# Moving operands of both products in areas of their own, at other offsets, and three output buffers in place of four

## The chip, the cores and the metric

The kernel runs on one NeuronCore of a Trainium2 chip. The metric is the device time of one execution in microseconds (us); lower is better. A time is the median of several runs. Profiles are of one execution, taken by the hardware profiler; its span, from the first to the last instruction, is a little shorter than a timed run.

## The reference

Windowed attention with a linear bias for each head, followed by a two-layer network with a squared Relu:

```
def _attn_ref(q, k, v):                  # 8 batches, 8 heads, 576 tokens, 64 values per head
    scores = scale * np.matmul(q, k.transpose(0, 1, 3, 2))
    rel = pos[:, None] - pos[None, :]
    bias = slopes[:, None, None] * (-np.abs(rel))[None, :, :]
    mask = (rel >= 0) & (rel < 128)
    attn = softmax(np.where(mask, scores + bias[None], -1000000000.0))
    return np.matmul(attn, v)

x = attn_out.transpose(0, 2, 1, 3).reshape(4608, 512)
h = np.maximum(x @ w_in, 0.0)            # w_in: 512 x 2048
out = h * h @ w_out                      # w_out: 2048 x 512
```

## The kernel before

The 4608 tokens are cut into nine chunks of 512 (`c` from 0 to 8). A chunk's attention output is made as four tiles of 128 values by 512 tokens, one for each pair of heads (`p`). The network then runs over 16 blocks of 128 hidden values (`f`).

**The two products.** Each is done in float32r with operands split into a high and a low part, three matmuls for one product: high x high, high x low, low x high. `gemm1(c, f)` (matmul at line 194) multiplies the four input tiles of the chunk by weight block f: 4 x 3 = 12 matmuls of 128 x 128 weights by 512 moving columns, into the one PSUM bank `g`. ScalarE takes the Relu out of `g` into `r` (line 204), VectorE squares `r` (line 207), ScalarE rounds it to the high part `hh` (line 211) and VectorE writes what is left as the low part `hl` (line 213). `gemm2(c, f)` (line 223) multiplies `hh` and `hl` by the second weight block: for each of four output blocks `m`, three matmuls into the accumulator `acc[m]`, which stays open over all 16 values of f. TensorE goes through gemm1 of step n, then gemm2 of step n - 2, and so on; the attention of later chunks stands in between, at fixed steps.

**The moving operands.** In every matmul of both products the weights are the stationary operand; the moving one is a tile of 512 float32r columns, 2,048 bytes in each partition. For gemm1 these are the two halves of `xu`, a tile of `[128, 2, 512]` from a pool with eight buffers: the high part is written by a ScalarE cast (lines 301 and 477), the low part by a VectorE subtraction (lines 304 and 480). For gemm2 they are `hh` and `hl`, from a pool with three buffers of each. Pools lay their buffers one behind the other, so `xu` tiles are 4,096 bytes apart and the halves and the `hh` and `hl` tiles 2,048 bytes: all of them begin at the same place within 1,024 bytes (544 bytes past a multiple of it).

**The weights.** All 16 blocks stay in SBUF, high and low parts interleaved, so that a weight block of 128 columns is read with a step of 8 bytes from a range of 1,024. In blocks f = 0, 4, 8 and 12 the first two of the four blocks of gemm1 are stored apart, with a step of 16 bytes (`APART`).

**The output.** At f = 15, when an accumulator is complete, it is copied to an output tile `o` (line 229; VectorE for m = 0 and 2, ScalarE for m = 1 and 3), and a DMA of 256 KB writes it to HBM (line 230), on SP's queue except for the last one of the kernel, which ScalarE issues. The pool `op` of these tiles has four buffers.

**Order.** The first two chunks' worth of attention is ordered by a planner with due times (`Plan`); later steps by the tile framework's scheduler. SP's queue carries the loads of q, k and v, a round trip of the attention squares through DRAM (`way`, lines 317 and 322) and the output DMAs, in program order.

Of the kernel before, what the change touches and what calls it, by code (L numbers as in the profile page):

```python
# [9 lines left out]
F32 = mybir.dt.float32  # L10
F32R = mybir.dt.float32r
# [3 lines left out]
ALU = mybir.AluOpType  # L15
# [22 lines left out]
FIRST = 39  # L38
APART = lambda i, f, b: i == 0 and f % 4 == 0 and b < 2
CASTS = (0, 2, 15,)  # L40
COPIES = (3,)
SQUARES = (6,)
NORMS = (7,)
# [18 lines left out]
class Kern:  # L62
    def __init__(self, ctx, tc, qkd, vd, w1d, w2d, cstd, outd):
        self.tc, self.nc = tc, tc.nc
        self.qkd, self.vd = qkd, vd
        self.w1d, self.w2d, self.cstd, self.outd = w1d, w2d, cstd, outd
        ep = lambda name, bufs, **kw: ctx.enter_context(tc.tile_pool(name=name, bufs=bufs, **kw))
        self.c = ep("const", 1)
        self.ld = ep("ld", 3)
        self.tp = ep("tp", 3)  # L70
        self.pp = ep("pp", 2)
        self.sm = ep("sm", 6)
        self.xu = ep("xu", 8)
        self.hp = ep("hp", 3)
        self.op = ep("op", 4)
        self.dr = ep("dr", 4, space=bass.MemoryType.DRAM)
        self.sc = ep("sc", 1, space=PSUM)
        self.at = ep("at", 1, space=PSUM)
        self.g1 = ep("g1", 1, space=PSUM)
        self.ac = ep("ac", 4, space=PSUM)  # L80
        self.cst = self.c.tile([128, CST], F32, name="cst")
        self.ident = self.cst[:, 0:128]
        self.mask = self.cst[:, 128:192].bitcast(I32)
        self.never = self.cst[:, 192:256]
        self.raw, self.w = [None] * NF, [None] * NF
        self.nc.alloc_sbuf_tensor("arena", [128, NF * 2048], F32)
        self.arena = self.nc.sbuf_base - NF * 8192
        self.x, self.qk, self.v, self.h, self.pairs = {}, {}, {}, {}, {}
        at = lambda slot, name, shape: self.nc.alloc_sbuf_tensor_at(name, shape, F32, offset=self.arena + slot * 4096).ap()
        self.wide = [at(2 * (NF - 3), "wide", [128, H, 256])[:, 2 * p : 2 * p + 2] for p in range(NP)]  # L90
        self.room_t = [at(2 * (NF - 5) + n, f"tw{n}", [128, 4, 256]) for n in range(4)]
        self.start_banks = [self.ac.tile([128, 512], F32, name="acc") for _ in range(4)]
# [32 lines left out]
    def room(self, c, p, name, shape, offset):  # L125
        if (c, p) != (0, NP - 1):
            return self.ld.tile(shape, F32, name=name)
        at = self.arena + (NF - 1) * 8192 + offset
        return self.nc.alloc_sbuf_tensor_at(f"{name}_", shape, F32, offset=at).ap()

    def load_qk(self, c, p, sg):
        if sg == 0:
            self.qk[c, p] = self.room(c, p, "qk", [128, 1152], 0)
        to, of = self.qk[c, p], self.qkd[c, p]
        if c == 0 and sg == 0:
            to, of = (x[:, 0:768].rearrange("p (n t) -> p n t", n=2)[:, :, 0:256] for x in (to, of))
        else:
            a, e = (0, 640) if sg == 0 else (640, 1152)
            to, of = to[:, a:e], of[:, a:e]
        self.nc.sync.dma_start(to, of)  # L140
# [20 lines left out]
    def convert(self, f):  # L161
# [8 lines left out]
        yield  # L170
        (nc.gpsimd.tensor_copy if f in CASTS else nc.scalar.copy)(wh, flo)
        yield
# [13 lines left out]
    def gemm1(self, c, f):  # L186
        nc = self.nc
        xs = [self.x[c, p] for p in range(NP)]
        g = self.g1.tile([128, 512], F32, name="g")
        i = 0  # L190
        for cc in range(NCC):
            wl, wh = self.block(0, f, cc)
            for w, part in ((wh, 0), (wh, 1), (wl, 0)):
                nc.tensor.matmul(g, w, xs[cc][:, part], start=i == 0, stop=i == 11)  # L194
                i += 1
                if (c, f, i) == (0, 0, 9):
                    yield
        yield
        r = self.hp.tile([128, 512], F32, name="r", bufs=1)
        hh = self.hp.tile([128, 512], F32R, name="hh")  # L200
        hl = self.hp.tile([128, 512], F32R, name="hl")
        self.h[c, f] = hh, hl
        with self.tc.high_priority(offset=100):
            self.relu = nc.scalar.activation(r, g, AF.Relu)  # L204
        yield
        if c or f in SQUARES:
            nc.vector.tensor_tensor(r, r, r, op=ALU.mult)  # L207
        else:
            nc.scalar.activation(r, r, AF.Square)
        yield  # L210
        nc.scalar.copy(hh, r)  # L211
        yield
        nc.vector.tensor_tensor(hl, r, hh.bitcast(F32), op=ALU.subtract)  # L213
# [19 lines left out]
class Segment:  # L233
# [42 lines left out]
    def out(self):  # L276
        (self.nc.vector.tensor_copy if self.k in COPIES else self.nc.scalar.copy)(self.own, self.z)

# [17 lines left out]
    def high(self):  # L296
        K = self.K
        if self.sg == 0:
            K.x[self.c, self.p] = K.xu.tile([128, 2, 512], F32R, name="xu")
        self.u = K.x[self.c, self.p][:, :, 256 * self.sg : 256 * self.sg + 256]  # L300
        self.nc.scalar.copy(self.u[:, 0], self.X)

    def low(self):
        self.nc.vector.tensor_tensor(self.u[:, 1], self.X, self.u[:, 0].bitcast(F32), op=ALU.subtract)  # L304

# [46 lines left out]
class Couple:  # L354
# [118 lines left out]

    def high(self):
        G = self.both[0]
        self.u = self.K.x[G.c, G.p] = self.K.xu.tile([128, 2, 512], F32R, name="xu")
        self.nc.scalar.copy(self.u[:, 0], self.X)

    def low(self):
        self.nc.vector.tensor_tensor(self.u[:, 1], self.X, self.u[:, 0].bitcast(F32), op=ALU.subtract)  # L480

    def back(self):
        self.values()
# [125 lines left out]
def start(K):  # L609
# [31 lines left out]
    for k in range(8):  # L641
# [12 lines left out]
        P.add(n("z"), "PE", 0.9 * w, (n("n"),) + chain("z"), d - 3, G.turn, ("at", "zp", "pp"), "tw")  # L654
        P.add(n("o"), "DVE" if k in COPIES else "Activation", 0.6, (n("z"),), d - 2, G.out, None, "at")
        P.add(n("m"), "DVE", 0.62 if w == 1 else 0.36, (n("z"),), d + 1, G.also, None, "zp")
# [34 lines left out]
    for f in range(NF):  # L691
        d, last = CONV(f), ("w", f)
        g = K.convert(f)
        for i, (engine, us) in enumerate(CONVERT):
            if i == 3 and f in CASTS:
                engine, us = "Pool", 1.5
# [117 lines left out]
```

## Time and profile before

| | before |
|---|---|
| median of 3 runs | 955.9 us (955.64 to 956.43) |
| span of the profiled execution | 954.1 us |
| TensorE busy | 945.6 us (99%) |
| VectorE, ScalarE, GpSimd busy | 499.0, 417.5, 215.3 us |
| HBM read, written | 67.76 MB, 26.21 MB |

In the rows of the profile, PE is TensorE's matmuls, PEld its weight loads, DVE VectorE, ACT ScalarE, POOL GpSimd and SP SyncE; SPq and ACTq are the DMA issues of SyncE and ScalarE. A row of a group has its line, engine and operation, the tiles it writes and reads (out<-in), their shape and count, then busy time in us, the mean of one in ns, and the idle time of the engine ahead of it with what ended it. The duration of a matmul contains the time in which the next one is already running; what one of a stream costs is read from the distance of starts, or from the chain, where the next piece begins when the one before gives way.

### The profile page before, as it was taken

What the parts mean: (1) busy time and instruction counts of PE and PEld (TensorE: products, weight loads), DVE (VectorE), ACT (ScalarE), POOL (GpSimd) and SP (SyncE); (2) the same over time, 40 slices, a digit from 0 to 9 for tenths busy, and PEclk for the clock granted to TensorE, in tenths of its full rate; (3) what the DMA queues carried; (4) which work ended last, traced back from release to release, by engine and by line L of the source; (5) the groups of instructions that cost most, each with busy time, mean ns of one, the idle gap of its engine ahead of it and who ended that gap; (6) DMA issues with size and microseconds to landing.
All of it is one profiled execution on the core that took longest, in us unless ns stands there. A gap on an engine that the chain in (4) does not pass through costs nothing.

```text
span 954.1 us, 17229 instructions
## 1 busy us (share of the span) xinstructions
PE 945.6 (99%) x6388; PEld 795.7 (83%) x6392; DVE 499.0 (52%) x1334; ACT 417.5 (44%) x1107; POOL 215.3 (23%) x254
## 2 busy tenths in 40 slices
PE   9899999999999999999999999999999999999998
PEld 5688888888888888888888888888888888888886
DVE  6998864455545455444544454455555444433222
ACT  7898743333444444434433343344344343332222
POOL 4123331222222222222222222221212222220000
PEclk9999999999999999999999999999999999999999
DMA  9974423322433333222433232333422231111001
GB/s 348 404 274 153 146 68 119 83 66 66 124 85 83 84 88 107 73 77 73 128 83 83 74 110 72 83 83 92 119 71 72 72 96 45 45 45 45 1 1 44
DMA packets 72883, 95.10 MB, mean 100 GB/s; under 512 B 8032, under 2 KB 41952, under 8 KB 72800
## 3 DMA queue, kind: packets, MB, share of 16 engines
q1 hardware_dynamic: 72368, 93.36, 32.9%
q8 instruction: 50, 0.82, 0.4%
q10 hardware_dynamic: 432, 0.66, 0.2%
q14 instruction: 33, 0.27, 0.1%
HBM read 67.76 MB, written 26.21 MB: 98 GB/s over the span
## 4 chain that ended last, share of the span: by engine, by line
PE 95%; DMA 4%; ACT 0%; issue 0%; DVE 0%; SPq 0%; DVEq 0%
PE acc L223 42%; PE g L194 42%; PE at L338 6%; PE s L392 2%; PE g L392 2%; DMA raw<-in_dram 2%; DMA wide<-in_dram 1%; DMA qk<-in_dram 1%; PE at L392 0%; ACT raw L165 0%; ACT t L426 0%; PE acc L291 0%; ACT t L419 0%; ACT o L229 0%; DVE xu L304 0%
## 5 line engine op out<-in xcount | busy, mean ns | idle before, releaser
L194 PE MATMUL g<-xu,w 128*128 128x512 f32 x1728 | 423.2, 394 | 0.8 <-issue 0.8
L194 PEld LDWEIGHTS g<-xu,w 128*128 128x128 f32 x1728 | 344.1, 209 | 56.2 <-issue 1.7
L223 PE MATMUL acc<-hh,w 128*128 128x512 f32 x1152 | 385.9, 396 | 0.0
L223 PEld LDWEIGHTS acc<-hh,w 128*128 128x128 f32 x1152 | 223.9, 194 | 44.6 <-issue 2.4
L207 DVE TENSOR_TENSOR r<-r 128x512 f32<-128x512 f32 x129 | 104.4, 810 | 245.4 <-ACT r L204 244.2
L204 ACT ACTIVATE r<-g 128x512 f32<-128x512 f32 x144 | 85.9, 597 | 325.8 <-PE g L194 322.7
L223 PE MATMUL acc<-hl,w 128*128 128x512 f32 x576 | 226.6, 393 | 0.0
L326 POOL TENSOR_SCALAR_AFFINE_SELECT pp<-pp 128x512 f32<-128x512 f32 x128 | 107.1, 841 | 210.6 <-DMA pp<-way 171.6
L213 DVE TENSOR_TENSOR hl<-r,hh 128x512 fp32r<-128x512 f32 x144 | 109.4, 760 | 68.3 <-ACT hh L211 67.6
L262 POOL TENSOR_TENSOR t<-t,nm 128x512 f32<-128x512 f32 x64 | 82.8, 1294 | 263.5 <-DVE nm L259 155.9
L223 PEld LDWEIGHTS acc<-hl,w 128*128 128x128 f32 x576 | 112.0, 194 | 19.8
L251 ACT ACTIVATE t<-t,nm 128x128 f32<-128x128 f32 x256 | 100.0, 393 | 56.7 <-DVE nm L244 56.6
L211 ACT CAST hh<-r 128x512 fp32r<-128x512 f32 x144 | 89.0, 618 | 76.1 <-DVE r L207 74.5
L438 DVE COPY_PREDICATED t<-cst,s 64x256 f32<-64x256 int32 x100 | 44.5, 445 | 40.8 <-ACT t L426 22.4
L313 DVE STREAM_TRANSPOSE pp<-t 128x512 f32<-128x512 f32 x64 | 45.2, 707 | 38.7 <-POOL t L262 38.5
L338 PEld LDWEIGHTS at<-pp,v 128*64 128x64 f32 x1024 | 55.2, 137 | 11.2 <-issue 10.8
L338 PE MATMUL at<-pp,v 128*64 128x128 f32 x1024 | 63.0, 276 | 0.0
L244 DVE CUSTOM_DVE_ANT_0 t<-t,cst 128x128 f32<-128x128 f32 x256 | 59.0, 293 | 1.0
L251 ACT ACTIVATION_READ_ACCUMULATOR t<-t,nm 128x1 f32 x256 | 48.2, 188 | 0.0
L392 PE MATMUL s<-qk 64*64 64x64 f32 (+2 forms) x1168 | 46.3, 251 | 0.8 <-ACT raw L165 0.8
L392 PEld LDWEIGHTS s<-qk 64*64 64x64 f32 x1168 | 41.9, 133 | 1.0 <-ACT raw L165 1.0
L428 POOL MEMSET t<- 64x128 f32 (+1 forms) x44 | 9.9, 227 | 137.5 <-PE g L392 128.5
(63 smaller groups left out, 472.2 us busy)
## 6 DMA issues: line engine op xcount, KB each, us to landing
raw<-in_dram SPq DMA_DIRECT2D x32, 512.0 KB, 8.7
way<-pp SPq DMA_DIRECT2D x256, 64.0 KB, 1.8
pp<-way SPq DMA_DIRECT2D x64, 256.0 KB, 2.8
qk<-in_dram SPq DMA_DIRECT2D x32, 320.0 KB, 3.5
v<-in_dram SPq DMA_DIRECT2D x32, 320.0 KB, 2.9
qk<-in_dram SPq DMA_DIRECT2D x38, 256.0 KB, 4.1
out_dram<-o SPq DMA_DIRECT2D x35, 256.0 KB, 4.3
v<-in_dram SPq DMA_DIRECT2D x3, 256.0 KB, 4.9
```

Of the source, the lines that this page charges most:

```text
L194: nc.tensor.matmul(g, w, xs[cc][:, part], start=i == 0, stop=i == 11)
L204: self.relu = nc.scalar.activation(r, g, AF.Relu)
L207: nc.vector.tensor_tensor(r, r, r, op=ALU.mult)
L211: nc.scalar.copy(hh, r)
L213: nc.vector.tensor_tensor(hl, r, hh.bitcast(F32), op=ALU.subtract)
L223: nc.tensor.matmul(self.acc[m], w, h, start=(f == 0 and i == 0), stop=(f == NF - 1 and i == 2))
L244: self.nc.vector.tensor_tensor_reduce(self.t[:, m], self.t[:, m], self.K.nrel(2 * self.p + m // 2), -0.125, BIG, ALU.add, ALU.min, self.nm ...
L251: return self.nc.scalar.activation(self.t[:, m], self.t[:, m], AF.Exp, bias=nm[:, m : m + 1], scale=-1.0, accum_out=nm[:, 4 + m : 5 + m],)
L262: self.nc.gpsimd.tensor_tensor(self.t, self.t, self.nm[:, 8:12].unsqueeze(2).to_broadcast([128, 4, 128]), op=ALU.mult)
L326: nc.gpsimd.affine_select(to, self.own, pattern=[[-32 * sign, 4], [0, 4], [-sign, 32]], compare_op=op, fill=0.0, base=0, channel_multiplie ...
L338: self.nc.tensor.matmul(self.X[r, o : o + 128].rearrange("p (a c) -> p a c", a=4), v[:, 2 * sg + k, r], src[:, :, 2 * j + i], start=sg == ...
L392: mm = nc.tensor.matmul(to, qk[r, q0 : q0 + 64], qk[r, k0 : k0 + 64 * n], start=True, stop=True, skip_group_check=True,)
```

## The change

The `xu` pool goes. A raw area `xs` takes its place and that of `hh` and `hl`: eight slots of `XS` = 4,288 bytes for the input tiles, then six of `HS` = 2,208 bytes for the hidden ones. `new_x` puts the input tile of chunk c and pair p into slot (4c + p) % 8, and shifts it by `SHIFT[c]`; the low part begins 2,080 bytes behind the high part. `hh` and `hl` rotate over three places each, shifted by `SHIFT_H`. Since 4,288 is 4 x 1,024 + 192, 2,080 is 2 x 1,024 + 32 and 2,208 is 2 x 1,024 + 160, the tiles now begin at many different places within 1,024 bytes. Most begin at a multiple of 32 bytes; those of chunks 2 and 7 begin 16 bytes past one, those of chunk 8 begin 8 bytes past one, and `hl` in the first of its three places begins 16 past one. The number of buffers is as before, eight and three. The pool of output tiles has three buffers in place of four.

```
+SHIFT = (0, 0, 16, 32, 64, 96, 128, 48, 8)
+SHIFT_H = ((0, 16), (32, 64), (96, 128))
+XS, HS = 4160 + 128, 2080 + 128
...
-        self.xu = ep("xu", 8)
         self.hp = ep("hp", 3)
-        self.op = ep("op", 4)
+        self.op = ep("op", 3)
...
+        self.nc.alloc_sbuf_tensor("xs", [128, 2 * XS + 3 * HS // 2], F32)
+        self.xs = self.nc.sbuf_base - 8 * XS - 6 * HS
...
+    def new_x(self, c, p):
+        at = self.xs + (4 * c + p) % 8 * XS + SHIFT[c]
+        self.x[c, p] = [self.moving(f"xu{i}_{c}_{p}_", at + 2080 * i) for i in range(2)]
+
+    def moving(self, name, at):
+        t = self.nc.alloc_sbuf_tensor_at(name, [128, 520], F32R, offset=at // 32 * 32).ap()
+        return t[:, at % 32 // 4 : at % 32 // 4 + 512]
...
-                nc.tensor.matmul(g, w, xs[cc][:, part], start=i == 0, stop=i == 11)
+                nc.tensor.matmul(g, w, xs[cc][part], start=i == 0, stop=i == 11)
...
-        hh = self.hp.tile([128, 512], F32R, name="hh")
-        hl = self.hp.tile([128, 512], F32R, name="hl")
+        at, n = self.xs + 8 * XS, (16 * c + f) % 3
+        hh, hl = (self.moving(f"h{'hl'[i]}{n}_{c}_{f}_", at + (2 * n + i) * HS + SHIFT_H[n][i]) for i in range(2))
...
-        self.u = self.K.x[G.c, G.p] = self.K.xu.tile([128, 2, 512], F32R, name="xu")
-        self.nc.scalar.copy(self.u[:, 0], self.X)
+        self.K.new_x(G.c, G.p)
+        self.u = self.K.x[G.c, G.p]
+        self.nc.scalar.copy(self.u[0], self.X)
```

The order of the instructions is the same on all five engines; line numbers behind the edits grow by 12 or 13 (194 becomes 206, 223 becomes 235, 229 becomes 241, 204 becomes 216). What differs is what the output copies wait for. These rows are ScalarE's at the end of chunk 5, where the next chunk's gemm1 already runs, each with the semaphores that it waits for (DMAHW is that of a DMA queue); before:

```order
L204 ACTIVATE r<-g 128x512 [waits DVE_49,PE_49]
L229 COPY o<-acc 128x512 [waits DMAHW4_49,PE_49]
L211 CAST hh<-r 128x512 [waits DVE_49]
L229 COPY o<-acc 128x512 [waits DMAHW6_49,PE_49]
L204 ACTIVATE r<-g 128x512 [waits DVE_49,PE_49]
```

And the same rows of the changed kernel:

```order
L216 ACTIVATE r<-g 128x512 [waits DVE_49,PE_49]
L241 COPY o<-acc 128x512 [waits DMAHW6_49,DMAHW5_49,PE_49]
L223 CAST hh_6_1__6571<-r 128x512 [waits DVE_49]
L241 COPY o<-acc 128x512 [waits DMAHW4_49,DMAHW2_49,PE_49]
L216 ACTIVATE r<-g 128x512 [waits DVE_49,PE_49]
```

Nothing has moved; the two copies wait for other DMAs. Before, each waited for the DMA of its own block in the chunk ahead. Now the copy of block 3, the second one here, takes the buffer that block 0 of the same chunk has just filled, and waits for its DMA as well. The last rows of ScalarE, where the final copy and the final DMA stand, before:

```order
L204 ACTIVATE r<-g 128x512 [waits DVE_49,PE_49]
L211 CAST hh<-r 128x512 [waits DVE_49]
L229 COPY o<-acc 128x512 [waits DMAHW7_49,PE_49]
L229 COPY o<-acc 128x512 [waits DMAHW1_49,PE_49]
L230 DMA out_dram<-o 128x512 [waits DMAHW5_49,Activation_49]
```

And of the changed kernel:

```order
L216 ACTIVATE r<-g 128x512 [waits DVE_49,PE_49]
L223 CAST hh_8_15__8888<-r 128x512 [waits DVE_49]
L241 COPY o<-acc 128x512 [waits DMAHW0_49,PE_49]
L241 COPY o<-acc 128x512 [waits DMAHW2_49,DMAHW7_49,DVE_49,PE_49]
L242 DMA out_dram<-o 128x512 [waits DMAHW5_49,Activation_49]
```

The last copy has two more waits: for VectorE, which filled that buffer with block 0, and for block 0's DMA.

More of the change, by code (lines that the diff above doesn't have):

```diff
@@ L298, in high @@
         if self.sg == 0:
-            K.x[self.c, self.p] = K.xu.tile([128, 2, 512], F32R, name="xu")
-        self.u = K.x[self.c, self.p][:, :, 256 * self.sg : 256 * self.sg + 256]
-        self.nc.scalar.copy(self.u[:, 0], self.X)
+            K.new_x(self.c, self.p)
+        self.u = [x[:, 256 * self.sg : 256 * self.sg + 256] for x in K.x[self.c, self.p]]
+        self.nc.scalar.copy(self.u[0], self.X)
     def low(self):
-        self.nc.vector.tensor_tensor(self.u[:, 1], self.X, self.u[:, 0].bitcast(F32), op=ALU.subtract)
+        self.nc.vector.tensor_tensor(self.u[1], self.X, self.u[0].bitcast(F32), op=ALU.subtract)
     def squares(self):
@@ L475, in high @@
         G = self.both[0]
-        self.u = self.K.x[G.c, G.p] = self.K.xu.tile([128, 2, 512], F32R, name="xu")
-        self.nc.scalar.copy(self.u[:, 0], self.X)
+        self.K.new_x(G.c, G.p)
+        self.u = self.K.x[G.c, G.p]
+        self.nc.scalar.copy(self.u[0], self.X)
     def low(self):
-        self.nc.vector.tensor_tensor(self.u[:, 1], self.X, self.u[:, 0].bitcast(F32), op=ALU.subtract)
+        self.nc.vector.tensor_tensor(self.u[1], self.X, self.u[0].bitcast(F32), op=ALU.subtract)
     def back(self):
```

## The prediction

> **What bounds the kernel now.** I read the page from the top down: busy shares, granted clock, the chain that ended last, the groups.
>
> ```profile
> PE 945.6 (99%) x6388; PEld 795.7 (83%) x6392; DVE 499.0 (52%) x1334; ACT 417.5 (44%) x1107; POOL 215.3 (23%) x254
> PEclk9999999999999999999999999999999999999999
> PE 95%; DMA 4%; ACT 0%; issue 0%; DVE 0%; SPq 0%; DVEq 0%
> L194 PE MATMUL g<-xu,w 128*128 128x512 f32 x1728 | 423.2, 394 | 0.8 <-issue 0.8
> L223 PE MATMUL acc<-hh,w 128*128 128x512 f32 x1152 | 385.9, 396 | 0.0
> L223 PE MATMUL acc<-hl,w 128*128 128x512 f32 x576 | 226.6, 393 | 0.0
> ```
>
> TensorE is 99% busy at the full granted clock, makes 95% of the chain, and has almost no idle time ahead of its matmuls. So the time is the number of matmuls times their pace. Lines 194 and 223, the two products, hold 1728 + 1152 + 576 = 3456 of them, and these are exactly the matmuls whose moving operands the change relocates. What one of them costs is read from the chain in order of time, whose columns are start, duration, engine and line, in groups of twelve:
>
> ```profile
> 55.47 2.80 PE acc L223 x12
> 58.27 2.79 PE g L194 x12
> 61.06 2.76 PE acc L223 x12
> ...
> 546.16 2.98 PE acc L223 x12
> 549.13 2.79 PE g L194 x12
> 551.92 2.76 PE acc L223 x12
> ```
>
> There are two paces. The usual one is 2.76 / 12 = 0.230 us per matmul; after some attention blocks a group goes at 2.80 / 12 = 0.233. The 2.79 groups of line 194 are those whose first two weight blocks are stored apart, and a group behind them returns to 2.76. The 2.98 group also holds the switch from the attention matmuls. All buffers that these groups read are spaced by multiples of 1,024 bytes, so every moving operand stands at one place within 1,024 bytes, and no row of before can show directly what another place costs. What can be read is whether the pace answers to traffic in the same memory. These are three stretches of one 2.76 group each, with the busy time of the engines, granted clock, DMA share and GB/s:
>
> ```profile
> core 0: us, PE busy (x) PEld busy (x) DVE busy (x) ACT busy (x) POOL busy (x), PEclk, DMA share, GB/s
> 61.06:63.82 2.76, 2.76 (x14) 2.33 (x13) 2.76 (x3) 2.68 (x8) 2.06 (x4) 1.00 1.01 380
> 551.92:554.68 2.76, 2.76 (x14) 2.33 (x13) 2.27 (x6) 2.65 (x10) 1.04 (x1) 1.00 0.00 0
> 934.00:936.76 2.76, 2.76 (x14) 2.33 (x13) 0.00 (x0) 0.13 (x1) 0.00 (x0) 1.00 0.00 0
> ```
>
> With three other engines busy and 380 GB/s of DMA the twelve take 2.76 us; with nothing beside them they take 2.76 us. Whatever sets 0.230, it isn't a share of the memory that others take away.
>
> **The change part by part.** No instruction is added, removed or moved on any engine. Two things differ: addresses, and waits of the output copies.
>
> *Addresses of the 3456 moving operands.* The pace at the new places is not shown, so it is bounded from both sides. Above: if every group fell into the slower pace of the first row of the chain, 288 groups would lose 2.80 - 2.76 = 0.04 us each, 11.5 us. Below, the nearest faster row is the start-up's matmul on zeros with the same 512 columns:
>
> ```profile
> 20.99 0.59 PE L121 MATMUL g<-zero 128*128 128x512 bf16 x2
> 32.48 0.38 PE L121 MATMUL g<-zero 128*128 128x512 bf16 x1
> ```
>
> Two of them end 0.59 - 0.38 = 0.21 us after one, against 0.23, so at most 0.02 x 3456 = 69 us could go. I take 0, since the row nearest to this operation is its own, and its 0.230 stays through every load on the memory that the windows show.
>
> *Casts and subtractions that write these operands* (ScalarE and VectorE) keep their shapes. They are 44% and 52% busy and no line of theirs carries the chain; I cost them at nothing, with TensorE's stream as their cover.
>
> *One output buffer less.* With four buffers each of a chunk's four copies had its own; with three, the copy of block 3 uses block 0's buffer and waits for block 0's output DMA of the same chunk. That wait stands on ScalarE. In the last chunk nothing is left to cover it:
>
> ```profile
> 948.36 0.69 DVE L229 COPY o<-acc 128x512 f32<-128x512 f32 x1 [3.51 <-PE acc L223]
> 949.08 1.71 SPq L230 DMA_DIRECT2D out_dram<-o  x3
> ...
> 950.43 0.59 ACT L229 COPY o<-acc 128x512 f32<-128x512 f32 x1 [0.79 <-PE acc L223]
> 951.04 0.35 ACTq L230 DMA_DIRECT2D out_dram<-o  x1
> out_dram<-o SPq DMA_DIRECT2D x3, 256.0 KB, 2.0
> out_dram<-o ACTq DMA_DIRECT2D x1, 256.0 KB, 2.1
> ```
>
> Block 0's DMA is issued at 949.08 and lands 2.0 us later, at 951.08. Block 3's copy, which began at 950.43, can begin at about 951.1: **+0.7 us**, and its own DMA (2.1 us) and the end move with it. The DMA can't win this back, as 2.0 us is what block 0's takes with the queue empty ahead of it.
>
> In the chunks before the last the same wait stands in the middle of the stream. What is queued behind it on ScalarE is the next Relu (line 204), for which TensorE waits through the single bank g, and the copy itself frees the accumulator of block 3. The tightest place that I found is chunk 5, where block 0's output DMA is itself issued late, behind a reload of the attention squares on SP's queue:
>
> ```profile
> 663.00 0.59 ACT L229 COPY o<-acc 128x512 f32<-128x512 f32 x1
> 663.84 0.43 SPq L230 DMA_DIRECT2D out_dram<-o  x1
> out_dram<-o SPq DMA_DIRECT2D x1, 256.0 KB, 3.2
> 665.76 0.60 ACT L204 ACTIVATE r<-g 128x512 f32<-128x512 f32 x1 [2.17 <-PE g L194]
> 667.40 0.62 PE L223 MATMUL acc<-hh,w 128*128 128x512 f32 x2
> 668.32 0.62 PE L194 MATMUL g<-xu,w 128*128 128x512 f32 x2
> ```
>
> That DMA lands at 663.84 + 3.2 = 667.04, so the copy moves from 663.00 to about 667.1 and ends at 667.7. The second matmul of the row at 667.40 is the first one into block 3's accumulator, and was due at 667.63. The loss is between 0.05 us (667.68 - 667.63) and 0.5 us (0.28 from its weight load at 667.40, and one pace of 0.23 after it). I take **+0.3**. The Relu then runs from 667.7 to 668.3, just ahead of the row at 668.32, so it adds nothing more. In the other chunks the DMA lands earlier against the stream, so I count 0 there; if each of the seven others lost what chunk 5 can at most, it would be 3.5 us.
>
> **Sum.** The profiled execution spans 954.1 us, and the median of the runs is 955.9, 1.8 above it. 954.1 + 0.7 + 0.3 = 955.1; with the 1.8 that lies around the span, **956.9 us**, 0.1% slower. About 0.2% (1.9 us) is what a measurement of this kernel can tell from no change, so I call this the same.
>
> **The rivals.**
>
> *Starts off a boundary cost a step (slower).* Tiles of chunks 2 and 7 begin 16 bytes past a multiple of 32, those of chunk 8 begin 8 past, and one in three of the hl tiles 16 past. If such a start costs the step between the two paces, 0.04 / 12 = 3.3 ns per matmul, line 194 pays for 3 x 16 groups, 48 x 0.04 = 1.9 us, and line 223 for 192 matmuls, 0.6 us: 956.9 + 2.5 = **959.4**. It decides from 0.9 us on, that is from 1.2 ns per such matmul, where the sum passes 957.8. For it: the two paces show that a step of this size exists. Against it: no row has such a start. [...]
>
> *The slower pace holds on (slower).* Mixed starts within a group could keep the stream at 2.80, which today ends at the next 2.79 group. For all of line 194 that is 144 x 0.04 = 5.8 us, about **962.7**; for everything, 968.4. For it: with one set of addresses both paces are seen, and each lasts over several groups, so the pace has a memory and may be tipped. Against: most of the stream is at 2.76.
>
> *The moving reads collide with the weight reads (faster).* Weights and moving operands are read at the same time, at a fixed distance within 1,024 bytes; other distances would then end the collisions. Half of the matmuls faster by one step gives 1728 x 3.3 ns = 5.7 us, **951.2**; all of them at 0.21 would give the 69 us above. For it: 0.23 is more than the 0.21 of zeros. Against it: the moving stream keeps its pace when ScalarE, VectorE and DMA write into the same memory. And the weights stored apart, whose loads lengthen the mean of line 194 to 209 ns against 194 in line 223, cost those groups only 0.03 us:
>
> ```profile
> L194 PEld LDWEIGHTS g<-xu,w 128*128 128x128 f32 x1728 | 344.1, 209 | 56.2 <-issue 1.7
> L223 PEld LDWEIGHTS acc<-hh,w 128*128 128x128 f32 x1152 | 223.9, 194 | 44.6 <-issue 2.4
> ```
>
> [...]
>
> *The change doesn't separate anything*, since the places repeat by another length than 1,024 bytes: the same time as the forecast, and counted with it.
>
> **How the numbers follow.** Pace unchanged: 55% (nine tenths of it within 0.2%, the rest slower because more chunks than one lose at the new wait). Starts off a boundary: 13%, three quarters of it over the bound. Slower pace: 12%, nearly all over. Collisions gone: 20%, of which 17 are over 0.2% faster and 3 are eaten by the wait. So faster 17%, same 55%, slower 28%. The range runs from 953.5, a small part of the gain of the third rival, to 963.5, line 194 at the slower pace with something added; outside are about 12% below (large gains) and 5% above.
>
> **What would show it.** Groups of lines 206 and 235 (the new numbers of 194 and 223) at 2.76 us in all chunks confirm the main step; 2.80 in chunks 2, 7 and 8 alone shows the first rival, 2.80 everywhere the second, any group under 2.74 the third. The last copy on ScalarE should begin 0.7 us later against the last matmul, its release put down to an output DMA, and chunk 5 should show a gap of some tenths ahead of block 3. The prediction is wrong if the pace moves with the chunk, or if the copies' wait reaches TensorE in every chunk.

## The result and the profile after

| | before | changed |
|---|---|---|
| median of 3 runs | 955.9 us (955.64 to 956.43) | 962.84 us (962.78 to 962.88) |
| ratio, 95% interval | | 1.0072 (1.0052 to 1.0091) |
| span of the profiled execution | 954.1 us | 961.2 us |

The changed kernel is 0.7% slower. From the page of the changed kernel, busy time and granted clock, and the chain by engine:

```profile
PE 952.1 (99%) x6392; PEld 797.6 (83%) x6392; DVE 495.7 (52%) x1334; ACT 417.2 (43%) x1107; POOL 218.2 (23%) x254
...
PEclk9999999999999999999999999999999999999999
...
PE 95%; DMA 4%; ACT 0%; issue 0%; DVE 0%; SPq 0%; ACTq 0%; DVEq 0%
```

TensorE is still 99% busy at the full clock and still makes the chain, and nothing else became the bound. Its own busy time grew by 6.5 us with the same instructions (the trace of before lacks four matmul records), so they take longer or follow one another at greater distances. The chain of the changed kernel, in a stretch of the last chunk without attention, start, duration, tile and line:

```profile
881.08 2.78 PE acc L235 x12
883.85 2.82 PE g L206 x12
886.68 2.80 PE acc L235 x12
889.48 2.81 PE g L206 x12
```

Before, such a stretch stood at 2.76 group after group, but for the 2.79 of the groups with weights stored apart:

```profile
875.78 2.76 PE acc L223 x12
878.54 2.79 PE g L194 x12
881.33 2.76 PE acc L223 x12
```

Now it stands neither at 2.76 nor at 2.80: each group has its own value. Summing, over the whole trace, the time from the first start of a group to the first start of what follows gives 403.8 us for the first product before and 407.1 now (+3.4), 402.9 and 405.8 for the second (+2.9), and 142.4 both times for attention and the rest. The end makes up the remaining 0.8. These are the last pieces of the chain now:

```profile
948.31 6.30 PE acc L235 x27
...
954.63 0.70 DVE o L241
...
955.35 2.02 DMA out_dram<-o
...
957.52 0.59 ACT o L241
```

The chain leaves TensorE at 954.6 and goes through block 0's copy and DMA to block 3's copy, as the new wait has it. That copy begins 957.52 - 954.63 = 2.89 us behind block 0's; before, it was 950.43 - 948.36 = 2.07. So 0.8 us is the output buffer's, at the end. The other place is in the first steps of chunk 6, where chunk 5's blocks are copied out. In the chain, before and then changed:

```profile
665.72 2.76 PE acc L223 x12
```

```profile
669.49 2.96 PE acc L235 x12
```

And in the timeline of that group, with what released an engine in brackets:

```profile
670.84 0.59 ACT L241 COPY o<-acc 128x512 f32<-128x512 f32 x1 [4.25 <-DMA out_dram<-o]
...
671.17 0.82 PE L235 MATMUL acc<-hh__6518,w 128*128 128x512 f32 x2
671.32 0.60 ACT L216 ACTIVATE r<-g 128x512 f32<-128x512 f32 x1
```

The copy waits for an output DMA, and the pair of matmuls whose second one opens the accumulator of block 3 takes 0.82 in place of 0.62: 0.2 us. With 3.4 + 2.9 (which holds this 0.2) + 0.8 = 7.1 us the difference of the spans is told. Some 6 us of it are the pace of the 3456 matmuls, 1.8 ns each.

### The profile page after: what moved, and what is told of

The parts are those of the page before. It is cut to its first block, busy times and chain, and to the rows that moved or that the text cites. A ratio compares the mean times of both kernels' runs of the same rounds, so it can differ in the third digit from the quotient of the medians.

```text
span 961.2 us, 17235 instructions
## 1 busy us (share of the span) xinstructions
PE 952.1 (99%) x6392; PEld 797.6 (83%) x6392; DVE 495.7 (52%) x1334; ACT 417.2 (43%) x1107; POOL 218.2 (23%) x254
## 4 chain that ended last, share of the span: by engine, by line
PE 95%; DMA 4%; ACT 0%; issue 0%; DVE 0%; SPq 0%; ACTq 0%; DVEq 0%
PE acc L235 42%; PE g L206 42%; PE at L350 6%; PE s L404 2%; PE g L404 2%; DMA raw<-in_dram 2%; DMA wide<-in_dram 1%; DMA qk<-in_dram 1%; PE at L404 0%; DMA out_dram<-o 0%; ACT raw L177 0%; ACT t L438 0%; PE acc L303 0%; DVE o L241 0%; ACT t L431 0%
## 5 line engine op out<-in xcount | busy, mean ns | idle before, releaser
L219 DVE TENSOR_TENSOR r<-r 128x512 f32<-128x512 f32 x129 | 101.8, 789 | 253.6 <-ACT r L216 252.4
L404 PE MATMUL g<-qk 64*64 64x128 f32 (+1 forms) x400 | 35.5, 270 | 0.0
L270 DVE TENSOR_SCALAR nm<-nm 128x4 f32<-128x4 f32 x72 | 14.0, 195 | 27.3 <-ACT t L263 26.9
L404 PEld LDWEIGHTS g<-qk 64*64 64x64 f32 x400 | 23.9, 133 | 4.6 <-issue 4.6
L438 ACT COPY t<-g 64x256 f32<-64x256 f32 (+2 forms) x56 | 18.5, 338 | 18.1 <-PE g L404 17.5
L241 ACT COPY o<-acc 128x512 f32<-128x512 f32 x18 | 10.6, 588 | 35.4 <-DMA out_dram<-o 24.1
L256 DVE DVE_READ_ACCUMULATOR2_ANT nm<- 128x1 f32 x256 | 21.4, 84 | 0.0
L181 DVE SCALAR_TENSOR_TENSOR raw<-raw 128x1024 int32<-128x1024 int32 x16 | 21.1, 1320 | 0.3
L438 ACT COPY t<-s 64x256 f32<-64x256 f32 (+2 forms) x48 | 15.6, 333 | 12.7 <-DVE t L450 11.6
```

Source lines behind the costliest of these rows:

```text
L256: self.nc.vector.tensor_tensor_reduce(self.t[:, m], self.t[:, m], self.K.nrel(2 * self.p + m // 2), -0.125, BIG, ALU.add, ALU.min, self.nm ...
L404: mm = nc.tensor.matmul(to, qk[r, q0 : q0 + 64], qk[r, k0 : k0 + 64 * n], start=True, stop=True, skip_group_check=True,)
```

## The experiments

In each, the kernel is the changed one or the one before with the edit shown (its main lines alone). "Place" is where a moving operand begins within 1,024 or 256 bytes of its partition; before, it is 544, which is 32 within 256. By the program's addresses the weights begin at 128 (low part) or 132 (high part) within 1,024. "Settled" is the time of a group of twelve, first start to next first start, away from attention and from the weights stored apart.

**All operands at one place again.** The areas and the three output buffers of the change stay; the shifts go, and slots are 4,096 and 2,048 bytes apart, so that all begin at 544 again, or all at 800, which also is 32 within 256.

```
-SHIFT = (0, 0, 16, 32, 64, 96, 128, 48, 8)
-SHIFT_H = ((0, 16), (32, 64), (96, 128))
-XS, HS = 4160 + 128, 2080 + 128
+AT = 416
...
-        at = self.xs + (4 * c + p) % 8 * XS + SHIFT[c]
-        self.x[c, p] = [self.moving(f"xu{i}_{c}_{p}_", at + 2080 * i) for i in range(2)]
+        at = self.xs + (4 * c + p) % 8 * 4096
+        self.x[c, p] = [self.moving(f"xu{i}_{c}_{p}_", at + 2048 * i) for i in range(2)]
...
-        hh, hl = (self.moving(f"h{'hl'[i]}{n}_{c}_{f}_", at + (2 * n + i) * HS + SHIFT_H[n][i]) for i in range(2))
+        hh, hl = (self.moving(f"h{'hl'[i]}{n}_{c}_{f}_", at + (2 * n + i) * 2048) for i in range(2))
```

> The changed kernel with every moving operand put back to the place within 1,024 bytes that it had before (544), in the new areas and with three output buffers. Theory A, the many places cause the slower pace: groups of twelve go back to 2.76 us, and only the waits of the output copies stay, about 0.8 us at the end and 0.2 us in chunk 5, so 956.5 to 957.2 us. Theory B, something else of the change (the new areas, the buffer) slows the stream: near 962.8 us.

> As the run before, but with every moving operand at 800 in place of 544. Theory A1, what counts is that all stand at one place, whichever: 2.76 us for twelve, 956.5 to 957.2 us. Theory A2, what counts is the distance to the weights, which begin at 128: another pace in nearly all groups, 2.78 to 2.80 (960 to 968 us) or under 2.76.

All at 544: 957.09 us, 1.0011 (1.0001 to 1.0020) of before. All at 800: 957.04 us, 1.0009 (1.0000 to 1.0019). The chain of the first:

```profile
549.78 2.79 PE g L204 x12
552.57 2.76 PE acc L233 x12
555.33 2.76 PE g L204 x12
```

2.76 is back. The addresses alone make 1.0072 - 1.0011 of the time, about 5.8 us; the new areas and the output buffer together make the rest, about 1 us.

**One place for each chunk's input, the second product at 544 throughout.** The places of the first product by chunk:

```
+PLACE = (lambda p, i: 544, lambda p, i: 544, lambda p, i: 128, lambda p, i: 256, lambda p, i: 384, lambda p, i: 672, lambda p, i: 800, lambda p, i: 576, lambda p, i: 552)
```

> The second product's operands at 544 throughout; all eight input tiles of a chunk at one place, another one for each chunk: 544, 544, 128, 256, 384, 672, 800, 576 and 552 for chunks 0 to 8. Theory A1 (one place within a product is enough): groups of the first product at 2.76 us in chunks 1 to 7. Theory A2 (distance to the weights): chunks 2 to 6 differ from each other by 0.01 to 0.04 us a group. Starts off a boundary: chunk 8 alone is slower.

962.5 us (one run). Settled groups of the first product: 2.760 at 544, 800 and 576; 2.780 at 256; 2.796 at 128 and at 384; 2.806 at 672; 2.815 at 552. 128 and 384 give the same, as 544 and 800 do: the pattern repeats after 256 bytes. And the second product, whose operands had not moved, was slowed with it. In chunk 2:

```profile
306.93 2.79 PE acc L238 x12
309.72 2.80 PE g L209 x12
```

In chunk 7, with the first product at 576, it was the second alone that was slowed: 2.814, beside 2.760 for the first. So what a group costs isn't told by its own place alone.

**Two or more places within a chunk.** As before, but the low half of the input, or each pair, is displaced: in chunk 1 the low half by 32, in 2 by 64, in 3 by 256, in 5 by 512, in 7 by 8; in chunk 4 each pair by 64 more, in 6 by 256 more.

```
+PLACE = (lambda p, i: 544, lambda p, i: 544 + 32 * i, lambda p, i: 544 + 64 * i, lambda p, i: 544 + 256 * i, lambda p, i: 544 + 64 * p, lambda p, i: 544 + 512 * i, lambda p, i: 544 + 256 * p, lambda p, i: 544 + 8 * i, lambda p, i: 544)
```

> The second product's operands at 544 throughout; input tiles by chunk: 1 to 3 with the low part 32, 64 and 256 bytes further than the high part, 4 with a step of 64 from pair to pair, 5 with the low part 512 further, 6 with a step of 256 from pair to pair, 7 with the low part 8 further, 8 all at 544. Theory A1: chunk 8 at 2.76 us and the mixed chunks at 2.77 to 2.81. Theory A2: chunks that mix places between two products of one place cost by the places they use, not by the mixing.

959.94 us (one run). Chunk 1, low half displaced by 32, and chunk 3, by 256:

```profile
196.20 2.80 PE g L209 x12
199.00 2.80 PE acc L238 x12
...
402.37 2.76 PE g L209 x12
405.13 2.76 PE acc L238 x12
```

Displacements of 256 and 512 (chunks 3, 5 and 6) cost nothing; 32, 64 and 8 do (2.80, 2.77 to 2.80, 2.77 in the first product). Again the period is 256. In chunk 1 the two places are 544 and 576, at each of which the first product alone was at 2.76 in the run before; mixed, they give 2.80.

**All operands at another place.** If only the steps between places cost, any common place should be as good as 544. So all at 672 (160 within 256), which is the edit of the first experiment with the area 128 bytes further on; and all at 552, 8 bytes past a multiple of 16, where the hidden tiles are 2,304 apart.

```
-AT = 416
+AT = 544
```

> As the run with all operands at 800, now at 672, a place that is another one within 256 bytes (160 in place of 32). Theory S, only steps from one place to another within 256 bytes cost: 2.76 us for twelve and 956.5 to 957.4 us in all. Theory D, the distance to the weights within 256 bytes sets the pace, and 32 is a good one: 2.78 to 2.82 us nearly everywhere, 960 to 968 us.

> All operands at 552, 8 bytes past a multiple of 16. Theory S: 2.76 us for twelve, 956.5 to 957.4 us. If a start off a boundary costs by itself: each group 0.01 to 0.04 us more, 960 to 968 us.

All at 672: 966.46 us, 1.0106 (1.0089 to 1.0123). All at 552: 971.45 us (one run). Their chains, first 672:

```profile
554.56 2.82 PE g L204 x12
557.38 2.80 PE acc L233 x12
```

And 552:

```profile
560.51 2.80 PE acc L233 x12
563.31 2.83 PE g L204 x12
```

The theory that only steps cost fell: with every operand at one place the stream goes at 2.80 all the way, even right behind the group with weights stored apart (2.82), where before returns to 2.76. At 552 the second product has the same 2.80, while the first has 2.83.

**Single steps out of the good place.** All at 32 within 256; only the hidden tiles of f = 5 and f = 10 are displaced, by another length in each chunk.

```
+STEP = (0, 32, 64, 96, 128, 160, 192, 224, 16)
...
+        at = self.xs + 8 * 4096 + n * HS + STEP[c] * (f in (5, 10))
```

> All operands at one place within 256 bytes, except hh and hl of f = 5 and f = 10, which stand 32, 64, 96, 128, 160, 192, 224 and 16 bytes further in chunks 1 to 8. Theory S with memory: the group of f = 10 and the five behind it, whose own operands are at the common place, go at about 2.80 us in some of these chunks, until the weights stored apart bring 2.76 back; about 957 to 959 us. Without memory: only the groups of f = 5 and 10 themselves and the one behind each change. Theory D: only those groups themselves.

959.42 us (one run). The chain behind f = 10, in chunk 2 (displaced by 64) and in chunk 5 (by 160); the displaced group itself is the first row of each piece:

```profile
321.31 2.79 PE acc L235 x12
324.10 2.79 PE g L205 x12
326.89 2.80 PE acc L235 x12
329.69 2.80 PE g L205 x12
...
630.72 2.80 PE acc L235 x12
633.51 2.76 PE g L205 x12
636.27 2.76 PE acc L235 x12
```

In chunk 2 the groups behind it read nothing but operands at the good place, and yet stay at 2.80, until the next group with weights stored apart. So it was behind displacements of 16, 32, 64, 96 and 128 at f = 10; behind 160, 192 and 224 the 2.76 came back by itself. **The pace has a memory.** The same operands at the same places go at either pace, according to what went ahead.

At f = 5 it went otherwise. There the displaced group stands right behind an attention block (but for chunk 8), and the group with weights stored apart right behind it. In chunk 5:

```profile
598.92 3.01 PE acc L235 x12
601.94 2.81 PE g L205 x12
604.75 2.80 PE acc L235 x12
```

The group stored apart takes 2.81, and the 2.80 goes on up to the next attention block. So it was with displacements of 32, 96, 160 and 192; with 16, 64, 128 and 224 the 2.76 was back behind that group. So weights stored apart don't always bring the fast pace back, and the length of a displacement doesn't tell by itself which pace follows: 160 and 192 led to 2.76 at f = 10, and to 2.80 here.

**No weights stored apart.** If those blocks are what brings 2.76 back, the kernel before must lose without them.

```
-APART = lambda i, f, b: i == 0 and f % 4 == 0 and b < 2
+APART = lambda i, f, b: False
```

> The kernel before with no weights stored apart (all with a step of 8 bytes). If the pace has memory: after the attention blocks 2.80 us for twelve lasts until the next block, up to seven groups more each time; 28 blocks with 7 x 0.04 us, less 36 x 0.03 for the groups that are no longer apart, about 7 us more than before, near 963. Without memory: about 1 us less than before, near 955.

963.25 us (one run), near the 963 expected. Its chain behind an attention block:

```profile
549.86 3.00 PE acc L223 x12
552.86 2.80 PE g L194 x12
555.66 2.80 PE acc L223 x12
558.46 2.80 PE g L194 x12
```

Before, the second row was a 2.79 group with weights stored apart, and 2.76 followed. Without it the 2.80 goes on. So it was behind 24 of the 28 attention blocks of chunks 1 to 7; behind the other four the fast pace came back by itself, as here:

```profile
446.92 2.97 PE acc L223 x12
449.90 2.76 PE g L194 x12
```

So at 32 within 256 most attention blocks leave the stream at 2.80, and the weights stored apart bring it back: in the kernel before, 2.76 follows behind them after all 28 of those blocks.

**Both products at one place, another in each chunk.** With this the table of places needs no mixing within a chunk:

```
+PLACE = (32, 0, 32, 64, 96, 128, 160, 192, 224)
...
+        at = self.xs + c % 2 * XA + PLACE[c] + 4096 * p
...
+        at = self.xs + 2 * XA + n * HS + PLACE[c]
```

> Both products' operands at one place within 256 bytes throughout a chunk, another one for each chunk: 32, 0, 32, 64, 96, 128, 160, 192 and 224 for chunks 0 to 8. Theory P, the place relative to the weights decides whether the stream comes back to its fast pace behind the weights stored apart: chunk 2 (32) at 2.76 us behind each of these, chunk 6 (160) at 2.80 throughout; some other chunks like the one and some like the other. Theory S, only steps cost: 2.76 us in all chunks, at the latest behind the second of the groups with weights stored apart.

962.96 us (one run). Settled groups, with the distance of the moving operand from the place where the weights begin (place - 128, within 256; for the high parts it is 4 less):

| place within 256 | 0 | 32 | 64 | 96 | 128 | 160 | 192 | 224 |
|---|---|---|---|---|---|---|---|---|
| distance from the weights | 128 | 160 | 192 | 224 | 0 | 32 | 64 | 96 |
| us for twelve | 2.78 | 2.76 | 2.76 | 2.79 | 2.80 | 2.80 | 2.80 | 2.80 |

Chunks 1 (place 0), 3 (64) and 5 (128) in the chain:

```profile
170.22 2.78 PE g L205 x12
...
378.78 2.76 PE acc L235 x12
...
582.30 2.80 PE g L205 x12
```

**The place, or the distance from the weights?** In the kernel before, 128 bytes are left free ahead of the weights, so that weights and moving operands both move by 128. The moving ones then stand at 672, where all of them were at 2.80 above, but as far from the weights as before.

```
+        self.nc.alloc_sbuf_tensor("space", [128, 32], F32)
         self.nc.alloc_sbuf_tensor("arena", [128, NF * 2048], F32)
```

> The kernel before with 128 bytes left free ahead of the weights, which moves the weights and everything behind them by 128: the moving operands are at 672, as in the run that took 966.5 us, and their distance to the weights is as before. Theory P with distance to the weights: as before, 955.9 to 956.6 us. Theory P with the place in memory itself: 2.80 us for twelve throughout and about 966 us less the waits of the copies, 965 us.

956.42 us, beside 956.39 for the kernel before (one run each). Its chain:

```profile
552.38 2.76 PE acc L224 x12
555.14 2.76 PE g L195 x12
```

2.76 at 672: so it is the distance between the two, and not the place itself. One thing doesn't fit into the table: all at 552 is a distance of 168, between the two fast ones, and there the second product stood at 2.80, beside a first product at 2.83. The runs don't tell why.

**A version that may beat both: place 64.** In the chunk at 64 above, the groups right behind attention were fast at once. The kernel before, with 32 bytes left free behind the weights, has all moving operands at 64 and the weights where they were; once as it is, and once without weights stored apart.

```
         self.arena = self.nc.sbuf_base - NF * 8192
+        self.nc.alloc_sbuf_tensor("space", [128, 8], F32)
```

> The kernel before (four output buffers, all moving operands at one place), with 32 bytes left free between the weights and everything behind them: the moving operands then start at 64 mod 256 instead of 32, the weights stay where they are; the order of the instructions is that of before. Theory (the place against the weights sets the pace, and at 64 the stream comes back to the fast pace by itself, as the chunk at 64 in the run with one place per chunk did): no slow groups behind the attention of a chunk. In the trace of before some 28 groups behind attention blocks stand about 0.04 us above the settled 2.760, and some 15 in the start phase; the 36 apart-stored groups cost 2.805 instead of 2.792 there. 43 x 0.04 - 36 x 0.013 = 1.3 us less: 954.0 to 955.5 where before shows 955.9. Rival (that chunk was fast for another reason, for instance the step with which it began): the pace is 2.80 in most groups, 957 to 963.

> The same with no weights stored apart (the 36 blocks whose high weights are 16 bytes from one another are stored as all others). Theory: at 64 the fast pace needs no reset, so the blocks only cost: each such group of 2.805 becomes 2.760, 36 x 0.045 = 1.6 us less than the run beside it, 952.5 to 954.5. Rival (the apart-stored blocks bring back the fast pace at 64 as they do at 32): 957 to 963, with groups of 2.80 from the first attention block on, as in the run of before without them (963.25).

955.57 us, 0.9996 (0.9987 to 1.0005), and 956.18 us, 1.0002 (0.9993 to 1.0011): neither can be told from before. Both times lie above what the theory expected, the first just so, and below what its rival did. In the first, the groups behind attention did get cheaper (most are 2.874 to 2.886, against 2.880 to 2.932 in before), the second product 0.9 us in all; but the groups with weights stored apart got dearer, 2.805 against 2.792, the first product 0.5 us in all, and attention and the rest 0.7. The second shows why 64 alone isn't enough; ahead of two of its attention blocks and behind each:

```profile
272.07 2.76 PE g L195 x12
274.83 2.76 PE acc L224 x12
...
289.13 3.02 PE acc L224 x12
292.15 2.80 PE g L195 x12
...
318.02 2.80 PE g L195 x12
```

In this stretch the stream is fast up to 287 us, then an attention block leaves it at 2.80, and it stays there behind the next block too; the one after that, at 341 us, leaves it at 2.76 again. The whole last chunk stays at 2.80. Both paces are possible at 64 too: behind 24 of the 28 attention blocks of chunks 1 to 7 it is at the fast one, where at 32, in the run without weights stored apart, it was so behind four. What the groups would save by needing no reset is about what those that stay slow cost.

## Why the prediction was right, and where it was wrong

The measured 962.84 us lies between the ends that the prediction gave (953.5 and 963.5), but not for the reason that it held to be the likeliest: its forecast was 956.9, 5.9 us less. The upper end had been set by a rival's price, and that this end was just high enough is in part luck, as is told below. By the prediction's own sign, "wrong if the pace moves with the chunk", its main step failed: the first product lost 0.33 to 0.48 us in chunks 1 to 7 and 0.75 in chunk 8. By its own steps:

- **What bounds the kernel** held: the stream of the two products, at the full clock, with nothing new on the chain but the output buffer's wait at the end. So did the casts and subtractions at nothing.
- **The addresses, taken as 0**, are the step that failed: "I take 0, since the row nearest to this operation is its own, and its 0.230 stays through every load on the memory that the windows show." The windows showed that traffic of other engines and DMA leaves the pace alone (2.76 us for twelve beside 380 GB/s and beside nothing), and that still stands. They could say nothing of the traffic that never varied there: TensorE's own weight loads, whose distance from the moving operand, taken within 1,024 bytes, differed by no more than 12 bytes in all of before. The runs put this term at about 5.8 us, half of the upper bound of 11.5.
- **The output buffer** held. The last copy moved by 0.8 us (+0.7 predicted), and block 3 of chunk 5 stalled TensorE by 0.2 (+0.3 predicted). Its copy, predicted to move to 667.1 on the old time, is at 670.84 with the group around it 3.77 later (669.49, against 665.72 for the same group in the chain of before): 667.07. That stall hangs on phases of tenths: with the same three buffers and all operands at 544 that group is 2.760, with no stall.
- **The rival "slower pace holds on"** is what happened, in part. Its argument, that both paces occur at one set of addresses and so have a memory that may be tipped, is confirmed by the single steps and by the run without weights stored apart. Its price for line 194 alone, 962.7, meets the measured 962.84 by luck, through another sum: both products lose, each about half of the step. For the changed kernel itself the runs give the pieces (places on either side, steps between them, memory); which of them makes which of its groups 2.78 or 2.82 was not taken apart.
- **The rival "starts off a boundary"** was wrong as priced. Chunks 2 and 7, with starts 16 past a multiple of 32, lost 0.33 and 0.35 us in the first product, no more than the others (0.33 to 0.48 in chunks 1 to 7). Chunk 8, 8 past one, lost 0.75, about 0.37 more than the mean of those seven, which is 1.9 ns for each of its 192 matmuls, beside the 3.3 of the price. But with everything at 552 the second product pays nothing for such starts beside the run at 672 (2.80 in both), and only the first does (2.83 against 2.80), so the starts themselves are not shown to be the cause.
- **The rival "collisions"** named the right quantity and had the wrong sign. The distance between moving operand and weights does bear on the pace, but before already stood at one of the two best distances tried, and no place went under 2.76. That reads collide is not shown: the runs vary addresses and don't see what is shared. What they show is that the pace depends on where the weights stand: with the moving operands at 672 it is 2.80 or 2.76, as the weights stand at 128 or at 256. Nothing of what the zeros' 0.21 seemed to promise was to be had at any place tried.

## What to carry to other kernels

Where a stream of matmuls sets the time and stands at one value group after group, the addresses of its operands can be part of that tuning: here they alone made about 5.8 us of 962.8. So a change of buffers has to keep their distance from the weights (here within 256 bytes) and from one another, or be measured. A pace that holds under the traffic of others, as the 2.76 did in the windows of before, says nothing of where the stream's own second operand stands, if that one never varied. And a group that looks costly, like the one with weights stored apart (2.79 in place of 2.76), may be what keeps the groups behind it fast (without it they stood at 2.80 behind 24 of 28 attention blocks): take it out in a run before calling it a cost.

## What the runs showed of the hardware

- One and the same stream of 128 x 512 float32r matmuls has two paces that last, 230.0 and 233.3 ns (2.760 and 2.800 us for twelve). In the last chunk of the run without weights stored apart all groups stay at 233.3; in that of before all stay at 230.0 but those with weights stored apart.
- Which one it falls to depends on the distance of the moving operand from the weights within 256 bytes. With one place for a whole chunk, 160 and 192 lead to 230.0, 0 to 96 to 233.3, and 128 and 224 to means of about 231.5 and 232.5; 168 (all at 552) is at 233.3 in the second product. Why 256, and what is shared, the runs don't show.
- At 160 and 192 both paces occur. Without weights stored apart the stream was at the fast one behind 4 of 28 attention blocks at 160, and behind 24 of 28 at 192.
- Moving operands at changing distances give settled values from 2.76 to 2.82 us for twelve, and 2.80 even where each place alone gives 2.76 (544 with 576); displacements by 256 and 512 bytes leave the 2.76 as it is.
- At a distance of 160, weights read with a step of 16 bytes in place of 8 bring the fast pace back behind every attention block of before in chunks 1 to 7 (2.79 for that group, 2.76 behind it), but not behind four of the displaced groups at f = 5. At a distance of 32 (all at 672) they don't: 2.82 for that group, and 2.80 behind it.
